# Causal attention and a token/channel mixer on one core: seven-product up projection for batches 1 to 3, single PSUM banks, casting loads at the start, and a written-out order

## The chip, the cores and the metric

The kernel runs on one core of a Trainium2 chip. The metric is the device time of one execution in microseconds (us). Of the kernel before there are three timed executions and one profiled one. In the rows of the profile PE is the matrix engine, PEld its weight loads, DVE the vector engine, ACT the scalar engine, POOL the engine that issues software DMAs, and SP the queue that issues hardware DMAs.

## The reference, cut to what matters

Eight batches, eight heads of 64 columns, 576 positions. Attention is causal by blocks of 64 positions; its output, with the heads side by side as 512 columns, is the input x of a mixer with two layers, one over positions and one over channels.

```python
scores = scale * np.matmul(q, k.transpose(0, 1, 3, 2))
scores = np.where(block_i >= block_j, scores, -1000000000.0)
attn = softmax(scores)
x = np.matmul(attn, v)                       # per batch 576 x 512
h = np.maximum(x.T @ w_tok1, 0.0) @ w_tok2   # 576 -> 256 -> 576 positions
u = x + h.T
h2 = np.maximum(u @ w_ch1, 0.0) @ w_ch2      # 512 -> 1536 -> 512 channels
out = u + h2
```

## The kernel before, in words

Everything is computed in bf16 with sums in PSUM. The program first makes a list of 1564 steps (`P.add`): each has the engines that may do it, a cost, the steps that it depends on, the PSUM banks that it takes and gives, and a function that issues its instructions. `Plan.run` then walks a simulated clock and puts the steps in an order; two tables, `SHIFTS` and `ONLY`, shift each step's rank and fix the engine of some. The instructions are issued in that order, so every engine's queue is fixed when the kernel is built.

The steps by stage:

- `load_qk` brings k and q in and transposes them in squares of 32 on DVE (L540). For batch 0 each of the nine pieces is loaded in fp32 by SP (L524) into the tiles that later hold gT, cast to bf16 by ACT or DVE (L498, L500), and then transposed. For the later batches POOL issues one load each of k and q of a half of the heads, which casts on the way (L517). `load_v` loads v by POOL (L566).
- `raise_clock` fills the time before the first data with matmuls on zeros: 16 of 512 columns (L469), then up to 110 of 256 columns (L476), of which the planner keeps those for which PE has nothing else.
- `score_set` (L664) computes a third of the scores of four heads as 64 or so small matmuls on parts of the array. `exp` (L682) turns them into weights, one ACT instruction for a pair of banks (128x1024). The pairs are two double banks, `sc01` and `sc23`; the other four of the eight PSUM banks are single ones (`mm`). When the last scores are done, the pairs are given back as four single banks (`late`).
- `head_out` (L712, L732, L738) and `ends_out` (L765, L787, L793) multiply weights by v and divide by the sums.
- `token_up`, `token_mix` (L906, L910, L1001, L1016): the layer over positions, giving u, then its transpose uT.
- The channel layer's first product, "up", gives gT, 1536 x 512 for each batch. `channel_up` (L1125) does it plainly: 12 groups of four 512-column matmuls, each group ended by one relu (L892 on ACT or L894 on DVE). `channel_up_half` (L1194) does it by blocks with seven products in place of eight, and `channel_up_fast` (L1318) does so for two batches together. Both form four differences of uT on DVE (L1166, L1284), copy sums between banks or to SBUF (L498, L500), add kept sums (L1233, L1351) and clip (L1246, L1248). Before, batches 0 to 3 go plainly, batches 4 to 7 by the fast form, and the last 64 positions of all batches, gathered as a ninth block, by the half form.
- The second product, "down" (L1452, fold L1476, sums L1434), is in the seven-product form already, except in batch 0 (`first_down`, L1547).

The choice is one line, and its use another:

```python
HALF_UP, FAST_UP = 4, 4
...
elif p >= HALF_UP:
    g_done = channel_up_half(p, uT_done, wc1_ready, 10 * p + 2)
else:
    g_done = channel_up(p, uT_done, wc1_ready, 10 * p + 2)
```

`cover` issues one more 512-column matmul when a bank that a copy is to fill came from the kind of bank whose words may not all have been written.

Of the kernel before, what the change touches and what calls it, by code (L numbers as in the profile page):

```python
# [11 lines left out]
FP32 = mybir.dt.float32  # L12
# [9 lines left out]
class Op:  # L22
# [3 lines left out]
        "engines", "cost", "deps", "emit", "prio", "take", "give", "xfer",  # L26
        "users", "need", "key", "waiting", "ready", "start", "end", "engine", "n", "mode", "at", "urgent", "until", "quick", "stick",
# [3 lines left out]
class Plan:  # L31


    LAG = {"PE": 0.28, "ACT": 0.2, "DVE": 0.18, "POOL": 0.22, "SP": 0.1}


    FIRST = {"POOL": 2.2, "ACT": 0.7, "SP": 0.7}
# [6 lines left out]
        for pool in pools  # L44
    }
# [8 lines left out]
    def add(  # L54
        self, engines, cost, emit, deps=(), prio=0.0, take=(), give=(), xfer=None, mode=0, at=0.0,
        urgent=0, until=1e9, quick=False, stick=False,
    ):

        o = Op()
        o.engines = (engines,) if isinstance(engines, str) else tuple(engines)  # L60
        o.cost = cost if isinstance(cost, dict) else {e: cost for e in o.engines}
        o.emit, o.prio, o.take, o.give, o.xfer = emit, prio, take, give, xfer
        o.mode, o.at, o.urgent, o.until, o.quick, o.stick = mode, at, urgent, until, quick, stick
        o.deps = list({id(d): d for d in deps if d is not None}.values())
        o.users, o.n = [], len(self.ops)
        self.ops.append(o)
        return o
# [4 lines left out]
    def fits(self, o, coming=()):  # L72
        for pools, n in o.need:
            have = sum(p in pools for p in coming)
            for p in pools:
                have += len(self.free[p])
            if have < n:
                return False
        return True

    def placed(self):

        letters = {"A": "ACT", "D": "DVE", "P": "POOL"}
        shifts, only = [int(x) for x in SHIFTS.split()], "".join(ONLY.split())
        assert len(self.ops) == len(shifts) == len(only)
        for o, shift, letter in zip(self.ops, shifts, only):
            o.prio += 0.05 * shift
            if letter in letters:
                o.engines = (letters[letter],)
        return self.run()  # L90

    def run(self):
        for o in self.ops:
            o.users = []
            o.need = [
                (pools, sum(set(other) <= set(pools) for other, _ in o.take)) for pools in {pools: 0 for pools, _ in o.take}
            ]
        for o in self.ops:
            o.waiting, o.ready = len(o.deps), o.at
            for d in o.deps:  # L100
                d.users.append(o)
        busy = {e: 0.0 for e in self.LAG}
        queued = [(o.at, o.n) for o in self.ops if not o.waiting]
        heapq.heapify(queued)

        avail = {e: [] for e in self.LAG}
        t, hard, soft, gives, order, mode = 0.0, 0.0, 0.0, [], [], 0
        left = len(self.ops)
        landed = [0.0] * 8

        fleeting = max([o.until for o in self.ops if o.until < 1e9], default=0.0)
        over = False
        while left:
            while queued and queued[0][0] <= t:
                o = self.ops[heapq.heappop(queued)[1]]
                o.key = (-o.urgent, o.prio, o.n, o)
                for e in o.engines:
                    bisect.insort(avail[e], o.key)
            while gives and gives[0][0] <= t:
                _, name, slot = heapq.heappop(gives)  # L120
                self.free[name].append(slot)
            began = False
            if not over:
                over = t > fleeting
                left -= sum(a[3].until < t for a in avail["PE"])
                avail["PE"] = [a for a in avail["PE"] if a[3].until >= t]
            for e in ("PE", "ACT", "DVE", "POOL", "SP"):
                if busy[e] > t or e == "POOL" and landed[-8] > t:
                    continue
                at = None  # L130
                tiled = e == "PE" and mode > 0
                for n, a in enumerate(avail[e]):
                    if a[3].stick > tiled or at is not None and not a[3].stick:
                        continue
                    if self.fits(a[3]):
                        at = n
                        if a[3].stick or not tiled:
                            break
                if at is None:
                    continue  # L140
                o = avail[e][at][3]
                soon = t + 0.6 * o.cost[e]
                if any(
                    r < soon and self.ops[n].urgent > o.urgent and e in self.ops[n].engines
                    for r, n in queued
                ):
                    continue
                if any(
                    -u[0] > o.urgent and self.fits(u[3], [name for r, name, _ in gives if r < soon])
                    for u in avail[e][:at]  # L150
                ):
                    continue
                for x in o.engines:
                    del avail[x][bisect.bisect_left(avail[x], o.key)]
                left -= 1
                began = True
                for pools, note in o.take:
                    note["pool"] = next(p for p in pools if self.free[p])
                    note["slot"] = self.free[note["pool"]].pop(0)
                o.engine, o.start = e, t  # L160
                o.end = busy[e] = t + o.cost[e] + 0.22 * sum(self.bare(note) for _, note in o.take)
                if o.mode is None:
                    o.mode = mode
                if e == "PE" and o.mode != mode:
                    o.end = busy[e] = o.end + 0.1
                    mode = o.mode
                order.append(o)
                lag = self.LAG[e]
                if o.xfer is not None:
                    first = o.end + self.FIRST[e]  # L170
                    if e == "POOL":
                        soft = max(soft, first) + o.xfer
                    else:
                        hard = max(hard, first) + o.xfer
                        soft += o.xfer * (soft > first)
                    o.end, lag = (soft if e == "POOL" else hard), 1.3
                    if e == "POOL":
                        landed.append(o.end + lag)
                for note in o.give:
                    to = self.TURN.get((note["pool"], note.get("covers")), note["pool"])  # L180
                    heapq.heappush(gives, (o.end + lag * (not o.quick), to, note["slot"]))
                for u in o.users:
                    same = u.engines == (e,) and o.xfer is None
                    u.ready = max(u.ready, o.end + ((e != "PE") * 0.05 if same else lag))
                    u.waiting -= 1
                    if not u.waiting:
                        heapq.heappush(queued, (u.ready, u.n))
            if not began:
                times = [b for b in busy.values() if b > t]
                times += [q[0] for q in queued[:1]] + [g[0] for g in gives[:1]] + landed[-8:]  # L190
                t = min(x for x in times if x > t)
        return order


SHIFTS = """
# [68 lines left out]
ONLY = """  # L264
# [17 lines left out]
def kernel(  # L282
# [11 lines left out]
    nc = tc.nc  # L294
# [1375 lines left out]
```

## Time and profile before

| what | us |
|---|---|
| timed executions | 288.24, 288.83, 289.09 (median 288.83) |
| profiled execution, first to last instruction (span) | 285.7 |
| profiled execution's own time | not listed apart from its span |
| PE / DVE / ACT / POOL busy | 280.5 / 234.5 / 157.9 / 69.6 |
| PE weight loads busy | 188.2 |
| mean granted clock of PE | 0.999 |

The span counts from the program's first to its last instruction; what a timed execution has beyond it lies before and after. Busy time is the union of an engine's recorded instructions. Matmuls overlap in the pipeline, so a matmul recorded with 381 ns does not take PE 381 ns: how fast PE goes is read from the chain of waits in order of time, which gives a stretch and its number of matmuls.

### The profile page before, as it was taken

Reading aid. Unit: us, or ns where it says so; the run is one execution under the profiler, and the core shown is the slowest. Engines: PE = TensorE matmul, PEld = TensorE weight load, DVE = VectorE, ACT = ScalarE, POOL = GpSimd, SP = SyncE. Lnnn points to the kernel's source line nnn. Section 1 sums busy time; section 2 is a strip of 40 time slices with the busy share of each in tenths; the row PEclk is TensorE's granted clock in tenths of the full one; section 3 lists DMA queues with packets and bytes.
Section 4 is the critical chain, followed back from the end, with each engine's and each line's share of the span. In section 5 each row is a group of like instructions: output and inputs, shape, how many; then the busy total and the mean of one; then the engine's idle time right before and its main releaser. Section 6 shows DMA issues by size and latency. Waiting matters only on the chain.

```text
span 285.7 us, 9042 instructions
## 1 busy us (share of the span) xinstructions
PE 280.5 (98%) x3923; PEld 188.2 (66%) x3923; DVE 234.5 (82%) x498; ACT 157.9 (55%) x212; POOL 69.6 (24%) x118
## 2 busy tenths in 40 slices
PE   8999999999999999999999999999999999999994
PEld 3676556565566856547876567744588985568883
DVE  3775788885699998479988588799996998999883
ACT  5986857568877458766475846335751037650000
POOL 8774545622251171701171001000000000000000
PEclk9999999999999999999999999999999999999999
DMA  8999999997499699942989006220080340000344
GB/s 228 215 165 208 213 182 186 206 183 151 66 100 105 82 197 204 187 54 22 136 137 199 6 2 76 76 92 2 19 129 2 117 179 0 0 2 0 149 127 169
DMA packets 64775, 32.65 MB, mean 114 GB/s; under 512 B 53088, under 2 KB 55264, under 8 KB 64736
## 3 DMA queue, kind: packets, MB, share of 16 engines
q0 software_dynamic: 44032, 16.75, 51.6%
q1 hardware_dynamic: 20704, 15.34, 21.8%
q8 instruction: 30, 0.49, 0.7%
q14 instruction: 9, 0.07, 0.1%
HBM read 35.85 MB, written 9.44 MB: 158 GB/s over the span
## 4 chain that ended last, share of the span: by engine, by line
PE 96%; DMA 1%; DVE 1%; SPq 0%; ACT 0%; issue 0%
PE mm L1452 17%; PE mm L1125 15%; PE sc L664 11%; PE late L1452 9%; PE mm L712 8%; PE late L1318 7%; PE mm L1318 6%; PE mm L906 5%; PE mm L1001 4%; PE mm L1547 4%; PE mm L765 2%; PE mm L1194 2%; DMA gT<-in_q_dram 1%; PE mm L910 1%; PE late L1194 1%; PE mm L476 1%
## 5 line engine op out<-in xcount | busy, mean ns | idle before, releaser
L682 ACT ACTIVATE e_sb<-sc 128x1024 bf16<-128x1024 f32 x95 | 92.4, 1023 | 40.9 <-PE sc L664 40.2
L540 DVE STREAM_TRANSPOSE qk_sb<-qk_sb 128x288 int32<-128x288 int32 (+1 forms) x65 | 41.2, 695 | 7.2 <-ACT qk_sb L498 4.0
L1125 PE MATMUL mm<-uT,wc_sb 128*128 128x512 bf16 x192 | 45.5, 381 | 0.0
L566 POOL DMA_DIRECT2D vals<-in_v_dram x45 | 37.2, 841 | 16.3 <-PE mm L712 7.3
L664 PE MATMUL sc<-qk_sb 32*64 32x64 bf16 (+7 forms) x1260 | 34.8, 293 | 0.2 <-DVE qk_sb L540 0.2
L1125 PEld LDWEIGHTS <-wc_sb 128*128 128x128 bf16 x192 | 20.2, 115 | 17.2 <-issue 1.3
L1452 PEld LDWEIGHTS <-sums 128*128 128x128 bf16 x288 | 27.7, 98 | 4.1 <-issue 0.9
L1452 PEld LDWEIGHTS <-gT 128*128 128x128 bf16 x288 | 27.5, 98 | 3.8
L664 PEld LDWEIGHTS <-qk_sb 32*64 32x64 bf16 x1280 | 19.6, 104 | 14.2 <-issue 9.0
L894 DVE TENSOR_SCALAR gT<-mm 128x512 bf16<-128x512 f32 x25 | 17.2, 687 | 13.9 <-PE mm L1125 13.2
L738 DVE TENSOR_TENSOR x_sb<-mm,rinv 128x256 bf16<-128x256 f32 x64 | 26.2, 421 | 1.5
L712 PE MATMUL mm<-vals,e_sb 128*128 128x65 bf16 x640 | 27.0, 193 | 0.1
L712 PEld LDWEIGHTS <-e_sb 128*128 128x128 bf16 x640 | 23.8, 97 | 4.8 <-issue 1.2
L892 ACT ACTIVATE gT<-mm 128x512 bf16<-128x512 f32 x35 | 20.5, 604 | 8.6 <-PE mm L1125 4.0
L498 ACT COPY mm<-late 128x512 f32<-128x512 f32 (+1 forms) x15 | 8.4, 563 | 26.3 <-PE late L1452 16.5
L906 PE MATMUL mm<-x_sb,w_sb 128*128 128x512 bf16 (+1 forms) x88 | 17.0, 321 | 0.0
L1016 DVE TENSOR_TENSOR u_sb<-mm,x_sb 128x512 bf16<-128x512 f32 x24 | 15.3, 680 | 1.4 <-PE mm L1001 1.2
L1452 PE MATMUL mm<-wd_sb,sums 128*128 128x256 bf16 x132 | 16.4, 273 | 0.0
L1318 PEld LDWEIGHTS <-ws_sb 128*128 128x128 bf16 x96 | 9.4, 98 | 9.9
L517 POOL DMA_DIRECT2D qk_sb<-in_k_dram x14 | 7.7, 553 | 32.8 <-DVE qk_sb L540 24.0
L1001 PE MATMUL mm<-aT,w_sb 128*128 128x512 bf16 x56 | 14.1, 380 | 0.0
L1452 PE MATMUL mm<-wc_sb,gT 128*128 128x256 bf16 x108 | 13.3, 273 | 0.0
(165 smaller groups left out, 481.8 us busy)
## 6 DMA issues: line engine op xcount, KB each, us to landing
out_dram<-o_sb SPq DMA_DIRECT2D x14, 512.0 KB, 3.4
qk_sb<-in_q_dram POOLq DMA_DIRECT2D x14, 288.0 KB, 6.3
qk_sb<-in_k_dram POOLq DMA_DIRECT2D x14, 288.0 KB, 6.9
vals<-in_v_dram POOLq DMA_DIRECT2D x28, 128.0 KB, 6.5
out_dram<-o_sb SPq DMA_DIRECT2D x7, 256.0 KB, 3.3
wc_sb<-in_moe_w_ch_dram POOLq DMA_DIRECT2D x8, 192.0 KB, 8.1
wc_sb<-in_moe_w_ch_dram POOLq DMA_DIRECT2D x3, 512.0 KB, 11.4
gT<-in_k_dram SPq DMA_DIRECT2D x4, 288.0 KB, 4.0
```

What stands on the lines that cost most here:

```text
L540: nc.vector.transpose(dst[:, 0:S, :] .rearrange("p s e -> p (s e)") .bitcast(I32) .rearrange("p (a k) -> p k a", k=NB)[:, k0:k1], raw2.bit ...
L566: nc.gpsimd.dma_start(out=t[128 - p : 128, J, hs, 0:64], in_=src)
L664: nc.tensor.matmul(out=home(n)[64 * half : 64 * half + 64, c : c + w], lhsT=bar[r, 0] if j is None else kT[i][r, 64 * j : 64 * j + 64, par ...
L682: nc.scalar.activation(dst, sc[SC.index(note["pool"])][:, :, 0:n], EXP, scale=scale)
L712: nc.tensor.matmul(out=u[:, I, 0:65], lhsT=e[:, h, c : c + 128], rhs=vt[:, J, head, 0:65], start=(J == 0), stop=(J == I),)
L738: nc.vector.tensor_tensor(out=xt[:, 0:4, 64 * head : 64 * head + 64], in0=u[:, :, 0:64], in1=ri[:, 0:4].to_broadcast([128, 4, 64]), op=MULT,)
L892: nc.scalar.activation(dst, src, RELU)
L906: nc.tensor.matmul(out=ps, lhsT=w1_sb[:, c, tt : tt + 255 : 2], rhs=xt[:, c, cols], start=(c == 0), stop=False)
L1001: nc.tensor.matmul(out=bank_of(bank), lhsT=w2_sb[:, t, 128 * si : 128 * si + 128], rhs=at[:, t, :], start=(t == 0), stop=(t == NDT - 1),)
L1125: nc.tensor.matmul(out=bank_of(bank), lhsT=wc1_sb[:, m, channels(cc)], rhs=uT[b % 2][:, :, m, :], start=(m == 0), stop=(m == NDM - 1),)
L1318: nc.tensor.matmul(out=bank_of(bank), lhsT=x(m), rhs=y[:, :, m, :], start=first and m == 0, stop=m == 1, skip_group_check=not first,)
L1452: nc.tensor.matmul(out=bank_of(bank)[:, 256 * i : 256 * i + 256], lhsT=x[:, kk, 128 * i : 128 * i + 128], rhs=y[:, kk], start=first and i ...
```

## The change

The planner goes out; the order of all steps, their engines and their banks are written out as one list, `ORDER`. A word of it is a step's number, the engine (T for PE, A for ACT, D for DVE, P for POOL, S for SP), and the letters of the banks it takes (a to d are `mm`, e to h are `late`, s and t the pairs). Steps are numbered as they are added; 1 to 18 are batch 0's loads and transposes of k and q, 19 to 28 its loads of v, 41 and 42 on are the matmuls on zeros, 171 is the first score set, 499 to 547, 663 to 711 and 830 to 878 are the up projections of batches 1, 2 and 3.

Four things change in the steps themselves. `HALF_UP` becomes 1, so batches 1 to 3 go through `channel_up_half`. From batch 1 on a score set takes four single banks, and each head has its own 128x512 exponential. The first k and q come by POOL loads that cast, with no staging and no cast instruction. The reciprocals of each head have their own buffer (9 in place of 4). The list also moves the memsets at the start from POOL to DVE, and the first ACT instruction (step 0, which loads the table of functions) to a place far behind.

```diff
-    HALF_UP, FAST_UP = 4, 4
+    HALF_UP, FAST_UP = 1, 4
...
-    rinv = ring(4, [128, 5, 1], FP32, "rinv")
-    stage = [t.rearrange("p c s -> p (c s)").bitcast(FP32) for t in gT]
+    rinv = ring(9, [128, 5, 1], FP32, "rinv")
...
-        fill("POOL", "bar", -1e6 + 1, (bar[:, 0, :], -BARRED), (bar[:, 1, :], 1.0))
+        fill("DVE", "bar", -1e5 + 1, (bar[:, 0, :], -BARRED), (bar[:, 1, :], 1.0))
...
                 if first:
-                    def emit_load(o, k0=k0, k1=k1, hbm=hbm, st=st):
-                        nc.sync.dma_start(out=st[:, D * k0 : D * k1], in_=hbm[:, D * k0 : D * k1])
...
-                        cast(o, raw2[:, D * k0 : D * k1], st[:, D * k0 : D * k1])
...
+                    def emit_load(o, k0=k0, k1=k1, hbm=hbm, raw2=raw2):
+                        nc.gpsimd.dma_start(out=raw2[:, D * k0 : D * k1], in_=hbm[:, D * k0 : D * k1])
...
-                notes = [{}, {}]
-                pools = [(SC[f : f + 1], notes[f]) for f in range(2)]
...
-                    these.append(exp(dst, 512, op, notes[f], prio + 0.1 * s, give=freed))
+                notes = [{"covers": True} for _ in range(4)]
+                op = score_set(b, hg, s, range(4), ready[hg] + e_war, prio + 0.1 * s, [(BANK, x) for x in notes])
...
+                    def emit(o, dst=e[:, h, SCOL[s] : SCOL[s] + 512], x=x):
+                        nc.scalar.activation(dst, bank_of(x), EXP, scale=scale)
...
+ORDER = """
+    1P 37D 39D 29D 41Ta 7P 30D 3P 5P 9P 15P 13P 19P 8D 2D 17P 4D 11P 6D 152P 10D 42Td 35D 21P 171Tsbc 196Tt 22P 14D
+    190A 43Ta 44Ta 45Ta 197A 16D 20P 46Ta 47Ta 48Ta 49Ta 50Ta 18D 51Ta 23P 52Ta 53Ta 172A 194Tt 12D 250P 54Ta 55Ta
...
+    588A 465D 471D 519Td 506A 590P 500D 504Th 521A 583P 501D 509T 576D 520A 522Tf 591P 505A 502D 524T 580P 523D 510A
...
```

The third line of `ORDER` shown is a part of the up projection of batch 1 (499 to 547) with steps of later batches between. Counted over the whole list, the three up projections of batches 1 to 3 give DVE 12 differences, 18 additions, 4 copies between banks, 3 copies to SBUF, 7 clips and 5 relus, and ACT 14 copies between banks, 6 copies to SBUF, 13 relus and 2 clips. Of the matmuls on zeros 29 of 256 columns remain, one of them ahead of the first score set.

More of the change, by code (lines that the diff above doesn't have):

```diff
@@ L1 @@
-import bisect
-import heapq
 import math
@@ L25 @@
     __slots__ = (
[L26 to L27 removed]
+        "engines", "cost", "deps", "emit", "prio", "take", "give", "xfer", "engine", "n", "mode", "at", "urgent", "until", "quick", "stick",
     )
 class Plan:
[L34 to L37 removed]
     TURN = {
@@ L70, in bare @@
         return note.get("seed", False) and note["pool"] in ("mm", "late mm")
[L72 to L79, printed above, removed]
-    def placed(self):
[L83 to L192, printed above, removed]
```

177 lines of the change are left out of this document (125 added, 52 removed), and 65 rows, old and new, of the table SHIFTS.

## The prediction

> **What bounds the kernel now.** First the page: busy shares, then the chain that ended last.
>
> ```profile
> span 285.7 us, 9042 instructions
> ...
> PE 280.5 (98%) x3923; PEld 188.2 (66%) x3923; DVE 234.5 (82%) x498; ACT 157.9 (55%) x212; POOL 69.6 (24%) x118
> ...
> PE 96%; DMA 1%; DVE 1%; SPq 0%; ACT 0%; issue 0%
> ```
>
> The chain is 96% PE, but a busy PE need not be PE at its pace. So the chain in order of time, at three places: the start, an up projection of batches 1 to 3, and the one half-form up projection that exists already.
>
> ```profile
> 5.71 0.68 ACT qk_sb L498
> 6.42 1.40 DVE qk_sb L540 x3
> 7.85 0.26 PE sc L664
> ...
> 66.09 1.73 PE mm L1125 x8
> ...
> 115.00 1.73 PE mm L1125 x8
> ...
> 243.58 0.44 PE mm L1194 x4
> ```
>
> From 7.85 us on nearly everything in the chain is PE. Eight 512-column matmuls take 1.73 us, 0.216 each; four of 256 columns take 0.44 us, 0.109 each. Both are the same pace per column, wherever they stand, so PE works at its pace and does not wait. The end of the span is the last matmul, a fold of 0.42 us on DVE, and an output DMA of some 3.4 us (the page's row of output DMAs).
>
> Next, how much room DVE and ACT have, in the stage of batches 1 to 3 and in later ones. The columns are stretch, length, then busy us (and count) of PE, PEld, DVE, ACT, POOL, the clock, and DMA.
>
> ```profile
> 60.00:180.00 120.00, 119.93 (x2201) 79.63 (x2199) 97.68 (x231) 81.72 (x99) 31.92 (x51) 1.00 0.88 110
> 190.00:250.00 60.00, 60.00 (x404) 40.84 (x403) 55.64 (x93) 27.82 (x47) 0.00 (x0) 1.00 0.22 56
> 250.00:268.00 18.00, 18.00 (x148) 14.32 (x146) 17.58 (x26) 4.15 (x7) 0.00 (x0) 1.00 0.08 30
> ```
>
> DVE is busy 81%, 93% and 98% of these, and PE is full in all three. Last the groups of instructions whose durations I need.
>
> ```profile
> L682 ACT ACTIVATE e_sb<-sc 128x1024 bf16<-128x1024 f32 x95 | 92.4, 1023 | 40.9 <-PE sc L664 40.2
> L894 DVE TENSOR_SCALAR gT<-mm 128x512 bf16<-128x512 f32 x25 | 17.2, 687 | 13.9 <-PE mm L1125 13.2
> L1233 DVE TENSOR_TENSOR gT<-late,half 128x512 bf16<-128x512 f32 x4 | 2.7, 684 | 0.0
> L831 ACT ACTIVATE e_sb<-mm 128x512 bf16<-128x512 f32 x2 | 1.2, 622 | 0.0
> ```
>
> **Up projection.** Three batches of 12 groups of four 512-column matmuls go: 144 x 0.216 = 31.1 us of PE. In come three batches of three groups of seven products of four 256-column matmuls: 252 x 0.109 = 27.5 us. PE saves 3.6 us. It all lies on the path, since PE is the chain. `cover` would add 0.216 us for each copied bank of the wrong kind (18 of them, 3.9 us, at worst). Following the bank letters through the list, each such bank was given back in between by a step that had covered it, so I take none.
>
> **What DVE gets.** In the list's up projections of batches 1 to 3 DVE has 12 differences (L1166 takes 0.42 us), 18 additions (0.684), 4 + 3 copies (L500, 0.69), 7 clips (L1248, 0.42) and 5 relus (0.687): 5.0 + 12.3 + 4.8 + 2.9 + 3.4 = 28.4 us. It loses the 15 relus that L894 has between 60 and 180 us, 10.3 us. Instructions in a row overlap in the records: the three transposes from 6.42 us have durations of 0.72, 0.46 and 0.42 us, 1.59 together, and take 1.38, so each of 35 more instructions costs some 0.09 less than its duration. Net 18.1 - 3.2 = +14.9 us. Of the 120 us of that stage PE needs 116.4 afterwards, and DVE's busy time goes from 97.7 to 112.6, which is 97%. That lies between the 93% and the 98% at which PE was not held up. Below, an exact fit costs nothing. Above, if DVE can't do better than the 93% of 190 to 250 us, the stage needs 112.6 / 0.93 = 121.1 us, 4.7 more than PE does. The mixture is nearer to the 98% row in load, but has attention beside it, where transposes and divisions come in bursts. I take +0.7.
>
> **Exponentials.** 84 instructions of 1.02 us become 168 of about 0.62: ACT +18.5 us by durations. With up's extra copies (35 instructions of 0.6 in place of 21, about +9) and the start's casts gone, ACT reaches about 183 of 282 us, 65%. The cover is ACT's waiting for scores (40.2 us in the L682 row). Without it each score set would come 0.2 us later, 42 x 0.2 = 8 us. A single bank comes free after 0.62 us rather than a pair after 1.02, which can only help PE; as PE did not wait for banks before, I count nothing.
>
> The Trainium skill, "Perfetto Trace Analysis", section "Optimizing Scalar/DVE Operations", speaks against this: larger operations pay when the engine is saturated. Here ACT is at 55%, so by its own condition it would not bite; if it did, the price is the 8 us above.
>
> **The start.** Now the last piece of q is cast from 6.95 us for 0.41, transposed, and PE starts its scores at 7.85. Afterwards POOL issues five loads of 0.55 us (the duration of L517) from 0.75 us on, when SP began; its memsets ahead are gone to DVE, which idles until 4.4 us. What a software load takes in that place no row shows. The quickest, k of a whole half (L517 at 65.86, nothing ahead of it), lands 3.7 us after its start; two such loads landed 1.8 us apart (45.5 and 47.3). So all five pieces, two whole loads, may be in at 0.75 + 3.7 + 1.8 = 6.3, at best a little below 6; then two transposes in 0.9 us: 7.2, a gain of 0.65. At the other end, the first v loads landed 6.7 us after issue (L566 at 2.85), while the hardware loads ran beside them: first data at 7.5 and scores at 9.5, a loss of 1.7. The hardware loads are gone afterwards, so the quick row is nearer. What is late next is v: its first five loads landed by 12.5 us and the first product of weights and v ran at 13.9. Afterwards they stand behind nine loads and a weight load on POOL; at 0.55 to 0.8 us each the last is issued at about 9.3 and lands, with the shortest 4.4 us of an L566, at 13.7. That eats a part: -0.4 net, between -0.9 and +1.7.
>
> The table load (1.28 us from 0.74) now precedes the first exponential; ACT has nothing else before 7 us and I count nothing, 1.28 if it waits for the scores first.
>
> **The rest.** The buffers of reciprocals remove waits of DVE for DVE, which its own order gives anyway: nothing. Two fewer zero matmuls fill time in which ACT sets the pace: nothing. The end keeps its last matmul, fold and DMA; the new order may move it by half a microsecond either way.
>
> **Sum.** Against the profiled span: 285.7 - 3.6 + 0.7 - 0.4 = 282.4. The profiled execution has no other time of its own; the median 288.83 is 3.1 us above its span, and I keep that: 285.5 us, 1.2% faster.
>
> **Rivals.**
>
> *DVE becomes the bound in the stage of batches 1 to 3 (ends slower).* Each of nine groups then waits in turn for copy, addition and clip, and scores wait for banks, which groups and score sets now share four by four. For it: 97% of DVE in a stage with bursts. Against: the half form at 225 to 244 us ran beside the fast form with DVE at 93% and cost PE nothing. It decides once DVE sustains less than 112.6 / 120 = 94%; at 89% the stage takes 126.5 us, +10.1 over PE's need, in place of my +0.7: 285.5 + 9.4 = 294.9; at 92%, 122.4 us and 290.8. I price it at 291.
>
> *PE has slack, and less work on it brings nothing.* The Trainium skill, "Trainium Kernel Development and Optimization", section "Performance Expectations", says that busy matmul time judges poorly how near PE is to its limit, and that weight-load busy time does better. In rows: PEld is busy 66%, so a third of PE's time would be waits drawn as pipelining, which stay; only the start's 0.4 comes, 288.4. Against: 0.216 and 0.109 us are the same pace per column in all stages, and no wait is in the chain between.
>
> *The first loads come late.* They take the 6.7 us of the v loads, +1.7 in place of -0.4: 287.6. For it: the same queue and engine. Against: fewer transfers beside them. The Trainium skill, "SBUF — State Buffer", the box on DVE blocking software DMAs, says that POOL can't write descriptors while DVE runs a two-port copy, and gives 3.1 us in place of 0.62 for a blocked load; an estimate by that page is +2.5 on one load. Here the L517 issues stay within 0.53 to 0.59 us over the whole kernel with DVE at 82%, which does not agree.
>
> **Chances.** Forecast 0.68; late loads 0.07; slack 0.10; DVE bound 0.15. What a measurement of this kernel can tell from no change is about 0.3%, 0.87 us: below 287.96 is faster, above 289.70 slower. Forecast and late loads end faster: 0.75. Slack ends the same: 0.10. DVE bound ends slower: 0.15. The forecast's own range is 282.5 to 287.5 (the start's -0.9, none of the +0.7 and an upside of the new order of 1 to 2; and above, half of the 4.7 for DVE). For 8 in 10 it goes up to 290.5, over the late loads, slack and the mild half of the DVE case, and down to 282.
>
> **What would show it.** Right: the rows of L1125 shrink to 48, L1194 grows to 336 at 0.109 us each in the chain, PE stays above 95% of it, DVE shows about 97% between 60 and 175 us, and the first score set starts near 7.3 us. Wrong: gaps on PE ended by L1233, L500 or L1248, or a chain that passes through DVE in that stage, would be the first rival; PE as full as before with a pace above 0.109 us per 256 columns the second; first scores after 8 us the third. A gain above 6 us would mean that the old order hid waits which the chain does not show.

## The result and the profile after

The change makes the kernel slower by 1.3%: 291.81 us median (290.37 to 294.22, 4 runs) against 288.6 us for the kernel before on the same chip (288.24 to 289.09, 4 runs), ratio 1.0128, 95% interval 1.0079 to 1.0177. The forecast was 285.5 us. All times are medians of every execution; the ratios, here and below, leave out executions more than 1.5% above the fastest of the same kernel.

The page of the kernel after: span, busy shares, the chain that ended last.

```profile
span 288.3 us, 9396 instructions
...
PE 279.3 (97%) x4029; PEld 198.2 (69%) x4029; DVE 240.7 (83%) x524; ACT 173.7 (60%) x317; POOL 72.2 (25%) x119
...
PE 70%; DMA 14%; DVE 8%; POOL 4%; issue 3%; ACT 0%; DVEq 0%; POOLq 0%; ACTq 0%
```

PE is still busy 97%, but the chain, which was 96% PE, is now 70% PE. DMA, DVE and POOL have come into it, so PE waits for others somewhere although its busy share hardly fell. The chain in order of time shows where:

```profile
2.48 4.50 DMA qk_sb<-in_k_dram
...
7.26 5.93 DMA w_sb<-in_moe_w_tok_dram
...
19.85 6.62 DMA qk_sb<-in_k_dram
...
26.49 1.26 DVE qk_sb L423 x2
27.75 0.27 DVE aT L777
...
104.52 1.75 PE mm L1077 x16
...
162.01 0.44 DVE x_sb L621
...
162.49 0.76 PE mm L595 x20
```

Up to 28 us the chain runs through POOL's software loads, one behind the other; the block products (L1077, 16 in 1.75 us) go at 0.109 us each, as forecast; and at 162 us PE waits for DVE. The longest waits of PE, first before 40 us in the kernel before, then in the kernel after, then from 150 to 175 us in the kernel after (in the kernel before there is none there). Columns: us in all, times, longest.

```profile
PE mm L469 <- DVE wd_sb L443: 1.2, 1, 1.2
PE sc L664 <- DVE qk_sb L540: 0.2, 1, 0.2
```

```profile
PE sc L547 <- DVE qk_sb L423: 1.4, 1, 1.4
PE mm L364 <- DVE wd_sb L338: 1.2, 1, 1.2
PE mm L595 <- DMA vals<-in_v_dram: 0.5, 1, 0.5
```

```profile
PE mm L595 <- DMA vals<-in_v_dram: 1.0, 1, 1.0
PE mm L595 <- DVE x_sb L621: 0.5, 1, 0.5
```

The 1.2 us is the wait of the zero matmuls for their zeros, the same in both kernels.

A sum over all matmuls separates work from waiting. Each recorded matmul counts with its columns at the pace of the chain (0.216 us for 512, 0.109 for 256; the zero matmuls count nothing); what is left of the elapsed time is "not useful". The work falls from 262.3 to 258.7 us, by 3.6 us. The level of both figures hangs by more than 10 us on the price of attention's small matmuls, which overlap; the differences between two kernels hardly do (within about 1 us). The not useful time, in us up to each moment:

| up to us | 10 | 20 | 30 | 60 | 150 | 170 | 190 | 280 |
|---|---|---|---|---|---|---|---|---|
| before | 8.8 | 13.8 | 14.4 | 15.0 | 18.3 | 18.6 | 19.4 | 19.4 |
| after | 8.9 | 14.7 | 17.0 | 18.4 | 22.2 | 24.3 | 25.2 | 25.9 |

After loses 2.6 us more than before by 30 us, 0.8 from there to 60, 0.5 from 60 to 150, 1.8 from 150 to 170, 0.8 behind that: 6.5 us. With -3.6 that is +2.9, and the last matmul indeed starts 3.0 us later (284.6 instead of 281.6).

### The profile page after: what moved, and what is told of

Same layout as the page of the kernel before. It is cut to its first block, busy times and chain, and to the rows that moved or that the text cites. A ratio compares the mean times of both kernels' runs of the same rounds, so it can differ in the third digit from the quotient of the medians.

```text
span 288.3 us, 9396 instructions
## 1 busy us (share of the span) xinstructions
PE 279.3 (97%) x4029; PEld 198.2 (69%) x4029; DVE 240.7 (83%) x524; ACT 173.7 (60%) x317; POOL 72.2 (25%) x119
## 4 chain that ended last, share of the span: by engine, by line
PE 70%; DMA 14%; DVE 8%; POOL 4%; issue 3%; ACT 0%; DVEq 0%; POOLq 0%; ACTq 0%
PE mm L1335 11%; PE late L1335 9%; PE late L1077 8%; PE late L1201 8%; DMA qk_sb<-in_k_dram 6%; PE mm L1077 5%; PE mm L1201 5%; PE mm L547 5%; DMA qk_sb<-in_q_dram 3%; PE mm L884 3%; DVE qk_sb L423 2%; PE mm L595 2%; PE late L789 2%; PE late L595 2%; DMA w_sb<-in_moe_w_tok_dram 2%
## 5 line engine op out<-in xcount | busy, mean ns | idle before, releaser
L754 ACT ACTIVATE e_sb<-late 128x512 bf16<-128x512 f32 x98 | 54.8, 607 | 18.0 <-PE late L547 13.5
L423 DVE STREAM_TRANSPOSE qk_sb<-qk_sb 128x288 int32<-128x288 int32 (+2 forms) x65 | 42.0, 698 | 8.7 <-DMA qk_sb<-in_k_dram 4.2
L754 ACT ACTIVATE e_sb<-mm 128x512 bf16<-128x512 f32 x70 | 39.7, 616 | 3.9 <-PE late L547 3.7
L1335 PEld LDWEIGHTS <-gT 128*128 128x128 bf16 x288 | 27.8, 98 | 4.9 <-issue 0.4
L547 PE MATMUL late<-qk_sb 32*64 32x512 bf16 (+7 forms) x648 | 28.6, 293 | 0.4 <-issue 0.2
L595 PEld LDWEIGHTS <-e_sb 128*128 128x128 bf16 x640 | 23.3, 97 | 5.7 <-issue 3.0
L547 PE MATMUL mm<-qk_sb 32*64 32x64 bf16 (+7 forms) x492 | 25.8, 288 | 0.0
L1077 PEld LDWEIGHTS <-ws_sb 128*128 128x128 bf16 x192 | 18.3, 98 | 3.9 <-issue 0.9
L595 PE MATMUL mm<-vals,e_sb 128*128 128x65 bf16 x380 | 17.1, 193 | 1.9 <-DMA vals<-in_v_dram 1.4
L621 DVE TENSOR_TENSOR x_sb<-mm,rinv 128x256 bf16<-128x256 f32 x38 | 15.9, 418 | 0.9
L1201 PEld LDWEIGHTS <-ws_sb 128*128 128x128 bf16 x96 | 9.3, 98 | 10.2 <-issue 0.2
L1077 PEld LDWEIGHTS <-wc_sb 128*128 128x128 bf16 x144 | 15.5, 114 | 1.1 <-issue 0.4
L1201 PE MATMUL late<-e_sb,ws_sb 128*128 128x512 bf16 x56 | 15.7, 379 | 0.0
L775 ACT ACTIVATE gT<-mm 128x512 bf16<-128x512 f32 x17 | 10.3, 624 | 8.5 <-PE mm L1201 3.8
```

The source lines that it names most:

```text
L423: nc.vector.transpose(dst[:, 0:S, :] .rearrange("p s e -> p (s e)") .bitcast(I32) .rearrange("p (a k) -> p k a", k=NB)[:, k0:k1], raw2.bit ...
L547: nc.tensor.matmul(out=home(n)[64 * half : 64 * half + 64, c : c + w], lhsT=bar[r, 0] if j is None else kT[i][r, 64 * j : 64 * j + 64, par ...
L595: nc.tensor.matmul(out=u[:, I, 0:65], lhsT=e[:, h, c : c + 128], rhs=vt[:, J, head, 0:65], start=(J == 0), stop=(J == I),)
L621: nc.vector.tensor_tensor(out=xt[:, 0:4, 64 * head : 64 * head + 64], in0=u[:, :, 0:64], in1=ri[:, 0:4].to_broadcast([128, 4, 64]), op=MULT,)
L754: nc.scalar.activation(dst, bank_of(x), EXP, scale=scale)
L775: nc.scalar.activation(dst, src, RELU)
```

## Experiments: which part costs it

Theories: L, the casting first loads on POOL's queue; D, DVE is the bound; O, the written order places loads and steps where PE waits. Each kernel is timed beside the kernel before, and ratios are against it.

**x1_hw_first**: after, with batch 0's keys and queries loaded by SP and cast on ACT and DVE, in after's order.

```diff
-                        nc.gpsimd.dma_start(out=raw2[:, D * k0 : D * k1], in_=hbm[:, D * k0 : D * k1])
+                        nc.sync.dma_start(out=st[:, D * k0 : D * k1], in_=hbm[:, D * k0 : D * k1])
```

> The kernel after, with the first k and q brought in as before: SP loads in fp32, casts on ACT (first half of the heads) and DVE (second half), then the transposes; the order is the same. Theory L (the first loads, put on POOL's queue, start late and push back the loads behind them; by 30 us the kernel after has lost 2.6 us more than the one before): 2 to 3.5 us below the kernel after (291.8), so 288.3 to 289.8, with the first score set near 7.9 us in place of 8.8. Theory D (DVE is the bound of the stage of batches 1 to 3): within 0.9 of the kernel after. Theory O (the written order itself places loads and waits badly, whatever brings the first k and q): the start is regained by 0.9 at most, 290.9 or more.

292.44 us, ratio 1.0114 [1.0081, 1.0147]: as slow as after. The first scores came at 9.49 us, not earlier: POOL's loads, no longer held up, ran beside SP's. So this isn't a clean undoing of the start.

**x2_before_sw**: before, with the casting loads and with the paddings filled by DVE (the reverse of that edit).

> The kernel before, with only its first k and q as casting POOL loads (no staging, no casts) and the memsets of the start on DVE. Theory L: 1 to 3 us slower than before (289.6 to 291.6), first scores at about 8.8 us. Theories D and O: the start alone, up to 0.9 slower, and no more.

288.35 us, ratio 0.9997 [0.9966, 1.0027]. The first scores moved from 7.85 to 8.57 us and the first up projection from 26.65 to 28.17, yet the time did not change: in before's order the loads cost less than the interval, 0.9 us either way. (In the one trace the last matmul does come 1.4 us later than in before's, 283.06 instead of 281.62; the ten timed executions don't show it.)

**x3_plain_up**: after, with each block product step of batches 1 to 3 doing plain 512-column matmuls instead, at the same places of the list.

```diff
+                        for m in ms:
+                            nc.tensor.matmul(
+                                out=bank_of(banks[to_]), lhsT=wc1_sb[:, m, channels(4 * k + n_)], rhs=ut[:, :, m, :],
```

> The kernel after, with the up projection of batches 1 to 3 done plainly within the same places of the order: 144 matmuls of 512 columns for 252 of 256, 12 relus per batch, no differences, no copies between banks, no clips. PE has 3.6 us more, DVE about 15 us less. If PE sets the pace apart from the stalls (theories L and O): 3 to 4 us slower than the kernel after, 294.8 to 295.8. Theory D: not slower than the kernel after, 291.8 or less.

294.74 us, ratio 1.0229 [1.0205, 1.0253]: 2.9 us over after. In after's own order the block products are worth most of the 3.6 us of the sum. That order was written for the block products, which may favour them.

**x4_less_dve**: after, leaving out the 12 differences and 9 clips of batches 1 to 3 (so the up projection's values differ).

> The kernel after, leaving out the 12 differences and 9 clips of the up projections of batches 1 to 3 (the products read parts of uT in their place): some 6.5 us less of DVE and 2 of ACT in that stage, PE the same. Theory D: 3 to 6 us below the kernel after, 286 to 289. Theories L and O: less than 1 us below it.

292.95 us, ratio 1.014 [1.0087, 1.0192], no faster than after, although DVE's busy time between 60 and 180 us fell from 107.2 to 101.1 us. D falls.

**x5_before_split**: before, with each exponential of a pair split in two of 512.

```diff
-            nc.scalar.activation(dst, sc[SC.index(note["pool"])][:, :, 0:n], EXP, scale=scale)
+            for h in range(2):
+                nc.scalar.activation(dst[:, h], sc[SC.index(note["pool"])][:, h, 0:n], EXP, scale=scale)
```

> The kernel before, with each exponential of a pair of banks issued as two of one bank; banks come free as before. It prices the smaller instruction alone. By the durations (0.61 for half of 1.02, 0.09 of it overlapped) ACT gets about 6 to 19 us, and has 40 us of waiting for scores: no change within 0.9 us. If ACT's chain at the start and between score sets is exposed: 1 to 8 us slower.

288.16 us, 1.0005 [0.9984, 1.0025]: the smaller exponentials cost nothing. Their banks come free in pairs here, so this does not test the single banks.

**w1_v6_early** puts the load 1007P, whose landing at 160.19 us ended a wait of 1.1 us, ahead of 1095P. **w2_v0_first** puts the weight loads 152P, 250P, 157P, 156P behind the value load 25P, which landed at 21.40 us and ended a wait of 0.64.

> The kernel after with one word of the order moved: 1007P, a load of v of batch 6, goes ahead of 1095P, a load of batch 7's q that stands some eight POOL steps earlier. In the kernel after it is issued at 152.4, lands at 160.2, and PE waits for it 1.1 us and then 0.6 for what follows. Theory O (the order loses time at single places where a load stands too far behind in POOL's queue): 1 to 1.8 us below the kernel after, about 290.3. A rival, by which the places only show a lateness that comes from elsewhere (another load, or DVE): within 0.5 of the kernel after.

> The kernel after with four words of the order moved: 152P, 250P, 157P and 156P (a weight load of the position layer, batch 1's q, two of the channel weights) go behind 25P, the last load of batch 0's v. Theory O: the 0.64 us for which PE waits for v at 21.4 goes, and the first product of the channel layer, at 29.96 in the kernel after, comes 0.6 to 1.2 us earlier: about 291. The rival (ACT's exponentials set the pace up to there): the same time as the kernel after within 0.4.

291.1 us (1.0102) and 293.12 us (1.0173). The first is at best 0.7 faster, inside the intervals. The load landed in time and its wait went, but the next wait, for DVE, grew from 0.67 to 1.56 us (from one matmul's start to the next):

```profile
163.37 0.42 DVE L621 TENSOR_TENSOR x_sb<-mm,rinv 128x256 bf16<-128x256 f32 x1
...
163.85 0.64 PE L595 MATMUL mm<-vals,e_sb 128*128 128x65 bf16 x16 [1.37 <-DVE x_sb L621]
```

PE went on 0.06 us behind DVE's multiplication. That came late because DVE's transposes ahead of it waited for a load of k that landed at 160.29 us (158.94 in after; w1's trace runs 1.2 to 1.6 us behind after's here). With the wait for v gone, PE only reached the wait for DVE sooner. The second is a miss: the wait at 21.4 us went, but the first up projection came at 30.10 us, no earlier than after's 29.96, and the kernel got slower, with a wait of 1.27 us at 125.9 us where after has one of 0.55, 100 us behind the edit.

## Experiments: other orders of the same steps

What remained was O. Two new orders for after's steps were made to be short in a replay of the list with the costs of before's planner.

> The steps of the kernel after, to the last one, in another written order: its order text alone is replaced, by one in which the first scores' waits, the late second-half value load of batch 0, the values of batch 6 and the projections of batches 1 to 3 are placed by the costs that the planner of the kernel before used. A replay of the written orders with those costs gives 290.0 us for the kernel after (on the chip 291.8), 284.1 us for the kernel before (on the chip 288.6) and 281.8 us for this order. Theory O (the steps save the 3.6 us and the written order gives more than that away): 281.8 plus an offset of 1.8 to 4.5 us, so 283.6 to 286.3 us, faster than before by 2 to 5 us; by 30 us of the span the time that is not useful matmul work is below 16 us (17.0 in the kernel after, 14.4 before), and no wait over 0.8 us is left between 150 and 170 us. Rival S (the steps themselves cost it: single banks, loads on POOL's queue and the extra DVE work leave no order that is better): 290.5 to 293 us, with the same waits at other places. Theory D (DVE's busy time): DVE is not relieved, so no gain either, 290 us or more.

> As the kernel with the first new order, but a second, independently found one, by the same costs 281.9 us: it tells whether the gain is one lucky order's. Theory O: 283.6 to 286.5 us, within 1.5 us of the first new order. Rival S and theory D: 290.5 us or more.

y1: 293.05 us (1.0148 [1.0098, 1.0197]). y2: 289.19 us (1.0018 [0.9989, 1.0046]). The same steps differ by 3.9 us between two orders to which the replay gives 281.8 and 281.9 (where PE's mean clock was 0.994 or more, y1 took 291.29 to 291.89 us; its three executions over 294 us had 0.987 to 0.991), and y2 loses from 60 to 150 us only 2.5 us (17.6 to 20.1), less than before's 3.3. So the order moves the time by as much as the change did, but not by the waits that the replay knows. y1's trace has jumps at single places where nothing that PE needed was late. One of them in the timeline (start, duration, engine, line, count, idle before):

```profile
54.82 0.51 PE L595 MATMUL mm<-vals,e_sb 128*128 128x65 bf16 x11
...
56.64 0.43 PE L595 MATMUL mm<-vals,e_sb 128*128 128x65 bf16 x9 [1.31 <-issue]
```

PE stops in the middle of a product of weights and v and waits 1.31 us for "issue", which is nothing that the profile shows. The page has one more queue:

```profile
q8 instruction: 31, 0.51, 0.7%
```

These are 31 packets of 16,384 bytes, and PE has 8,080 recorded matmul and weight-load instructions, 260 per packet: they bring PE's instructions. In y1 the sixth came from 54.32 to 55.25 us, and PE went on 1.39 us later. The stalls of that kind stand at PE's instructions number 447, 703, 1727, 2239, 3007, 4287 and 6077 to 6079 of the complete traces of after, y1 and y2: 191 and a multiple of 256, within two (before's small one stands four short of it). In the complete traces of before, after, y1 and y2 no block begins earlier than 1.28 us behind its packet's end. The table lists the stalls on which the argument rests (times in us; "entered" is when PE began the block before, and can be off by up to a microsecond in w1, w2, fb, fh and g, whose traces lack some 25 matmul records; a stall runs from start to start):

| kernel | entered | packet | PE goes on | behind packet's end | stall |
|---|---|---|---|---|---|
| before | 109.65 | 112.08 to 112.97 | 114.52 | 1.56 | 0.26 |
| after | 82.23 | 85.61 to 86.51 | 88.13 | 1.62 | 0.60 |
| after | 120.84 | 121.34 to 123.07 | 124.48 | 1.41 | 0.55 |
| w1_v6_early | 122.05 | 123.78 to 124.74 | 126.01 | 1.28 | 1.00 |
| w2_v0_first | 121.58 | 123.53 to 124.49 | 125.94 | 1.45 | 1.27 |
| y1_new_order | 51.46 | 54.32 to 55.25 | 56.64 | 1.39 | 1.51 |
| y1_new_order | 64.66 | 68.03 to 69.01 | 70.47 | 1.46 | 0.83 |
| y1_new_order | 170.13 | 174.60 to 175.70 | 177.05 | 1.35 | 1.72 |
| y2_new_order | 12.33 | 15.53 to 16.48 | 17.97 | 1.49 | 0.40 |
| y2_new_order | 17.97 | 21.37 to 22.31 | 23.62 | 1.31 | 0.48 |
| y2_new_order | 168.44 | 172.20 to 173.38 | 174.82 | 1.44 | 1.30 |
| fb_same_start | 119.70 | 124.52 to 125.48 | 126.72 | 1.24 | 3.43 |
| fh_before_start | 167.29 | 173.04 to 173.96 | 175.29 | 1.34 | 2.29 |
| g_moved_dma | 151.64 | 156.03 to 157.20 | 158.65 | 1.45 | 1.33 |

So: about when PE enters a block the next is fetched (the packet begins between 2.7 us before and 4.5 us behind that in the complete traces); in the rows above it was usable 3.6 to 8.0 us behind it; and where a block is all small matmuls, PE has used it up sooner (20 of L595 take 0.76 us in the chain above, so 256 instructions of that kind take an estimated 4.9 us). A packet's end alone proves nothing: w1's wait for DVE also ended 1.37 us behind one, but 44 instructions into a block. The stalls of y1 add up to 4.06 us, those of y2 to 2.18, and the spans of the two profiled executions differ by 2.0.

With this cost in the replay (next block 5.8 us after the last was entered while software loads run, 4.2 otherwise) it gave 289.5 us for y1 (span 289.5) and 286.9 for y2 (287.5), the two from which the cost was taken. Two orders written with it:

> The steps of the kernel after in a third written order, made with two costs that the first two new orders did not have: TensorE's instructions come in blocks of 256 (each matmul is two), and a block that is entered is followed by the next one 5.8 us later while software loads are in flight, 4.2 us otherwise, as the packets of the instruction queue and the stalls behind them show in the runs of before, after and the first two new orders (a stall ends 1.3 to 1.6 us behind the packet's end, at 55.25 -> 56.64 us in the first new order); and POOL's first load begins at 1.25 us. By these costs a replay gives 289.5 us of span for the first new order (on the chip 289.5), 286.9 us for the second (on the chip 287.5) and 282.1 us for this one. Theory F (the steps save 3.6 us; what a written order loses is waits that its maker did not price: instruction fetch, late loads, the start): a span of 281.5 to 284.5 us, a time of 283.5 to 286.5 us, faster than before by 2 to 5 us, with no wait over 0.5 us at a block boundary of the instruction stream. Rival S (the steps themselves cost what they save): 288.5 us or more. Rival: the fetch is no cause and the second new order was lucky: 289 to 293 us, with stalls at boundaries where the replay has none.

> As the third written order, but found from the first new order instead of the second: by the same costs 282.3 us of span. Theory F: a time of 283.5 to 286.5 us, within 1.5 us of the other. Rival S: 288.5 us or more. The first new order, from which it comes, took 293 us; if it stays within 1 us of that, the costs of fetch and start are not what set it.

z1: 288.18 us, ratio 0.999 [0.996, 1.0019]; z4: 289.24, 1.0 [0.9965, 1.0035]. No fetch stall over 0.5 us is left: the only waits of that length that end so behind a packet are for values that land just then (landing at 17.23 and going on at 17.27 us in z1, 16.95 and 17.00 in z4). z1 is 3.6 us below after, with the same steps, so after's loss against before is its order's; z4, which comes from y1, is 3.8 below that. But theory F's forecast (283.5 to 286.5) missed by 1.7 and 2.7 us. Rival S (288.5 or more) was nearer: z1 falls 0.3 short of it and z4 lies in it. And the replay, with the new cost, was 4.2 us below z1's span (282.1 against 286.3), so costs are still missing from it.

The traces of z1 and z4 show where the time goes. From the first up projection to the last matmul before takes 254.97 us (26.65 to 281.62), after 254.60, z1 251.34 (29.83 to 281.17) and z4 251.13. Behind the start, z1 and z4 are thus 3.6 and 3.8 us shorter than before, as much as the block products save; the start takes it away again, with a first up projection at 29.83 and 32.76 us (z4's has a half clock in it, see below). The casting loads, a part of the steps, belong to that start, so S is narrowed down to it and not refuted. These are single traces.

## Experiments: the start, and the block products once more

> The steps of the kernel after, but batch 0's first keys and queries come as in the kernel before (SP's loads into staging tiles, casts on ACT and DVE, paddings filled on POOL), in a written order of its own made with the same costs (first software load, instruction fetch); its replay gives 280.9 us, that of the third written order 282.1. Theory L2 (what is left against before, once the order is priced, is the start: by 30 us of the span 2.6 us more of not useful time than before's 14.4, from the casting loads): 285 to 286.5 us, 1.7 to 3.2 below the third written order, below before by 1.5 to 3.5 us, with the first scores by 8.2 us and 14 to 15.5 us not useful by 30 us. Rival (the loads cost nothing, as in the kernel before with casting loads): 287.5 to 288.7 us.

> As the one before it with an independently found order, replay 281.4 us: theory L2 285.3 to 287 us, the rival 287.5 to 289 us.

> The steps of the kernel after (casting loads, single banks) with the plain up projection in batches 1 to 3, in a written order of its own made with the same costs; its replay gives 282.8 us, that of the third written order (block products) 282.1. If the block products are worth their 3.6 us of TensorE work when each has an order of its own: 291 to 292 us, 3 to 3.6 over the third written order's 288.2. If the block products' own waits (DVE's differences, joins and clips, 36 more uses of a bank, and faster use of the instruction stream) take most of it back: 288.5 to 289.5 us. Theory O alone does not tell these apart, since in the order of after both stood in the same places.

301.69, 293.38 and 301.17 us: all far off, and not for the reasons under test. The windows of h2 (stretch, busy us of each engine, then the clock of PE):

```profile
5.50:12.30 6.80, 2.98 (x25) 1.69 (x23) 1.76 (x4) 2.34 (x4) 2.56 (x5) 1.00 1.18 285
12.40:32.80 20.40, 19.93 (x321) 13.34 (x318) 11.10 (x34) 12.77 (x16) 15.21 (x28) 0.50 1.33 172
```

PE was busy 2.98 of 6.8 us, and for the next 20.4 us its clock was granted at half. This order leaves PE idle ahead of the first scores (3.8 us, up to 11.85), and zero matmuls, which have no worth in the replay, don't fill it. In v4 the half clock lasts from 10.8 to 27.8 us, in z4's profile from 11.8 to 25.5. In h2 and h3 the loads of POOL had also moved ahead of its paddings and slowed SP's. These three tell nothing about loads or products.

Three more orders therefore keep a known start. fb and fp: after's first 16 us, with block products and with plain ones. fh: before's loads and before's first 16 us, with block products.

> The kernel after (block products, casting first loads, single banks) with its own order kept for the first 16 us, zero matmuls included, and the rest written anew with the costs of fetch and loads; replay 283.6 us. The start is after's, so the clock should be granted as in after (two earlier orders had let TensorE idle among the first scores, and the granted clock fell to 0.5 for 13 to 20 us). Theory O (what after loses behind its start is its order): 287.5 to 289.5 us, 2.5 to 4 below after's 291.8. Rival S: 290.5 us or more.

> As the one before it, but with the plain up projection in batches 1 to 3; the first 16 us are those of the kernel after too, the rest has an order of its own, made in the same way; replay 283.8 us. If the block products are worth 3 us or more in any order: 3 to 3.6 us above the one before it. If an order that suits each variant takes most of that back (the replays differ by 0.1): within 1 us of it.

> The steps of the kernel after with the first keys and queries loaded as in the kernel before (SP into staging tiles, casts on ACT and DVE, paddings on POOL), and with the order of the kernel before kept for the first 16 us, zero matmuls included; the rest is written anew in the same way; replay 283.1 us. Theory L2 (the casting loads cost after 2.6 us by 30 us of the span): first scores at 7.8 to 8.2 us, first matmul of the up projection by 28 us, 285 to 287 us, 2 to 3 us below the kernel with after's start. Rival (loads cost nothing; the order makes up for them): within 1 us of it.

fb 291.95 us (1.013 [1.0091, 1.017]), fp 291.22 (1.0103 [1.0082, 1.0125]), fh 289.92 (1.0052 [1.0025, 1.008]). As run, the block products are worth nothing when each variant has its own order. But three of fb's six executions (293.10 to 293.50 us) had a mean clock of 0.988, the others (290.22 to 290.79) 0.994 or more, and fb has one stall of 3.43 us, in the middle of a score set:

```profile
123.28 0.38 PE L547 MATMUL late<-qk_sb 32*64 32x448 bf16 x2
...
126.72 0.36 PE L547 MATMUL late<-qk_sb 32*64 32x448 bf16 x1 [3.06 <-issue]
```

and fp has none over 0.36. Without it fb's median would be 288.5, 2.7 below fp's, and its profiled execution 286.8, 4.3 below fp's 291.09; x3 had 2.9. That is a subtraction, not a run. With before's start the first up projection of fh comes at 27.52 us instead of fb's 29.65, and the time is 2.0 us lower. That agrees with a start that costs about 2 us, but fb's longer stall and lower clock are in the 2.0 as well, so it is not shown.

The last run asks whether the stall of fh is the fetch. It moves five transfers off the stretch from 162 to 171 us and leaves PE's instructions alone:

```diff
- 1113P 1114P 1116P (behind 1110P)   1002S 907S (ahead of 1098S)
+ 1113P 1114P 1116P (behind 1058P)   1002S 907S (behind 1099S)
```

> The kernel fh_before_start with five transfers moved and nothing else: three value loads of batch 7 go behind POOL's two tail steps (issued at 171 us instead of 162 to 164; their values are wanted at 183 us), and one crossbar transpose and one store go behind the next two transposes on SP (issued from 176 us instead of 163 to 165; wanted at 188 and 217 us). No instruction of TensorE changes or moves. In fh_before_start TensorE stood from 173.03 to 175.29 us at a block boundary of its instruction stream: it had entered the block before at 167.3, the packet of the next came only at 173.04 to 173.96, behind these transfers, and the clock was granted at 0.5 from 177.0 to 180.4. Theory F (the fetch waits behind the data transfers): the packet comes by 170.5 us, the stall of 2.26 us falls below 0.5, the clock stays at 1.0 there, and the time falls by 2 to 4 us, from 289.9 to 286 to 288 us, at or below before's 288.1. Rival (the stall has another cause, such as what TensorE waits for by semaphore): the stall stays within 0.5 us of 2.26 and the time within 1 us of 289.9.

290.85 us (1.0082 [1.0052, 1.0113]). PE's waits from 150 to 190 us, in fh and in g:

```profile
PE late L609 <- ACT e_sb L768: 2.1, 1, 2.1
```

```profile
PE late L662 <- DMA vals<-in_v_dram: 2.7, 1, 2.7
PE late L561 <- issue: 1.0, 1, 1.0
PE late L561 <- DVE x_sb L635: 0.4, 1, 0.4
```

The packet that came 5.75 us after the block before was entered (167.29 to 173.04) now comes 0.75 after (168.06 to 168.81), and the 2.1 us, which the profile had put down to ACT, are gone: the fetch had been behind the data transfers. But the last of the moved value loads, now beside two transposes, landed 8.2 us after its issue, at 181.91 us, and PE waited 2.7 us for it. And the 1.0 us for "issue" is a fetch stall again, at 158.65 us (in the table), at a block boundary that fh passed without one at 158.41. The mechanism held at the place of the edit; the forecast time did not.

## Why the prediction was wrong

- **Up projection, -3.6.** Right as work: 336 matmuls of L1077 at 0.109 us, 3.6 us less in the sum. In the time it shows as 2.9 in after's own order (x3); fb and fp, each with an order of its own, don't show it as run.
- **DVE, +0.7.** Near in size, by luck: the not useful time of 60 to 150 us grew by 0.5, and x4 gains nothing, but the 0.7 was taken for a DVE at 97%, and DVE was at 89%. It got busier by 9.5 us in its stage, not 14.9 (why is open; the prediction's 35 more instructions are 34 by its own counts, 0.1 us):

```profile
60.00:180.00 120.00, 118.16 (x2234) 88.58 (x2232) 107.20 (x246) 94.30 (x184) 33.32 (x54) 1.00 0.87 111
```

The rival that DVE becomes the bound named nearly the measured time (291), by a mechanism that x4 refutes.

- **Exponentials and reciprocal buffers, 0; table load, 0.** Right for the smaller exponentials (x5) and the table load (hidden at 0.76 us); the single banks and the reciprocal buffers were not run alone.
- **The start, -0.4.** The first step that failed. "All five pieces may be in at 0.75 + 3.7 + 1.8 = 6.3": the first issue began at 1.26 us, half a microsecond late, and the first piece landed 3.16 us later at 4.42, near the 4.45 of the sum because two errors cancel, but the last at 8.10. The 1.8 us, a distance of two loads in a quiet queue, was 3.7 for five pieces. The first scores came at 8.80 us, not 7.2. I had this as a rival, late loads, at +1.7 in place of -0.4, with a chance of 0.07, and its sign, first scores after 8 us, came; what it left out is what follows in the same queue: v's second half landed at 21.40 (a wait of 0.64), and the first up projection started 3.3 us late. By 30 us it is +2.6, outside the -0.9 to +1.7. (The 0.53 to 0.59 us held against a blocked load are times of issues, not of landings, and don't bear on it.)
- **The rest, "the new order may move it by half a microsecond either way".** The step that failed most. A whole order was replaced, and I priced it at its end only. Behind 30 us after lost 3.9 us more than before: two fetch stalls of 0.60 and 0.55, a value load of batch 6 issued 8 us ahead of its use and landing with it (1.1), DVE late behind a load of k that landed at 158.94 (0.6), and smaller ones. The medians of four orders of the same steps (after, y1, y2, z1) span 288.2 to 293.1 us; with the clock at 0.994 or more y1, the slowest, is at 291.3 to 291.9.

The sum's terms for the steps were mostly right, but the start was too hopeful and the terms of the order were missing. That the order made after slower than before is shown: z1, with the same steps, equals before. That the steps would bring the forecast 3 us in a good order is not: no order that I ran beats the kernel before, so rival S, that the steps cost what they save, is not refuted. The traces of z1 and z4 put what is lost into the start, where the casting loads are, but no time shows it. Whether the start of z1 could be had as early as before's, how much of fb's 3.43 us a better order would keep, and why before's order absorbs the casting loads of x2 stay open.

## What to carry to other kernels

A change that comes with a new hand-written order is two changes, and the order can be worth more than the edit: price it by its loads (issue, queue, landing, first use) and not at its end alone. When PE is the bound, stretches dense in small matmuls are exposed to instruction fetch, and transfers queued just there can make the fetch late (fh and g). Its marks are a wait in the middle of a product, for "issue" or an engine that had long been done, some 1.3 to 1.6 us behind a packet of the instruction queue, and a place at a multiple of 256 in PE's stream; w1 shows that without the place the other marks mislead. Zero matmuls that look like waste may hold the clock (no run tests it), so a search for an order needs a price for PE's idle time.

## What the runs showed of the hardware

PE's instructions come in packets of 16,384 bytes for 256 instructions, a matmul being two. The Trainium skill, "Runtime: NRT & Kernel Launch", section "Instruction fetch mechanics", gives the same block size, which the trace confirms; it also says that the cost of crossing a block's boundary is mostly hidden. The traces agree for most boundaries (28 of 30 in after, 27 of 30 in y1), but not for all: the others cost 0.26 to 3.43 us each, always ending 1.24 to 1.62 us behind the packet's end, with the packet 0.5 to 5.8 us after the block before was entered. In fh one came 5.75 us after that with five transfers in flight, and in g, with these moved, 0.75 us.

The granted clock fell to 0.50 after a sparse start for 3.41, 13.65, 17.07 and 20.48 us (w1, z4, v4, h2), and for 3.41 us after stalls of 2.1 to 3.1 us in h3, fh, g and v4 (not after 3.43 us in fb's profile, nor 2.1 in h2's): always multiples of 3.41 us. One such window costs an estimated 1.7 us of PE's work and 0.006 of the mean clock, which is the size of the steps between the executions of y1 and fb. The Trainium skill, "TensorE: Matmul & The Clock Gate", section "Part 1: The HAM clock gate (the "warmup" mystery)", gives a window of some 3.4 us of activity; the trace agrees.

POOL's software queue held eight loads at most; whether the chip or the program sets that, no run shows. In the kernel after, from 21 us on, issues follow the landing of the load eight issues earlier: landings at 21.40, 26.47 and 27.45 us, issues at 21.68, 26.75 and 27.74. That is why the chain runs from DMA to POOL to DMA there.
